# Ten pair tiles instead of eleven, under a newly written order table

## The chip, the cores and the metric

The kernel runs on one core of a Trainium2 chip. The metric is the device time of one execution in microseconds (us); lower is better. Five engines work side by side: PE (matrix products), DVE (vector operations), ACT (casts, copies, activations), POOL (almost unused here) and SP (which issues the DMA transfers).

## The reference

The input is 2048 rows of width 640 in float32. A layer of attention and a gated feed-forward network (FFN) are applied one after the other, each ahead of a residual sum:

```
h  = x + attention(layernorm(x)) @ wo       # 32 heads of 20; each row looks at 8 rows: itself and 2, 4, ... 14 back
h2 = h + (silu(n @ w_gate) * (n @ w_up)) @ w_down      # n = layernorm(h); 640 -> 1728 -> 640
```

## The kernel before

The rows are cut into four blocks of 512 (b = 0 to 3). Every float32 factor is split into a high and a low part (ACT casts the high part, DVE subtracts to get the low one), and each product is three passes of matmuls over them. So each operand costs DVE work before PE can use it.

Attention has no matmul for its logits and sums: the 16 pairs of block and head group are done on DVE. K, V and Q leave PE, are evicted by ACT into a staging tile `st` (L698), written to DRAM scratch (`ksc`, `vsc`, `qsc`, L711 to L727), and loaded back row-shifted into `kv` and `pq` (L742 and L747). DVE then multiplies (L755, L795), reduces (L760) and folds (L804), and SP writes the result to `osc` (L817).

The FFN's 1728 columns are 14 tiles of 128 (the last has 64). In the "classic" form a tile of one block is 30 matmuls of 512 columns for gate and up (L976; 15 for the last tile), SiLU on ACT (L1014), a product on DVE (L1015), a split (L1005 and L1007 or L1009) and 15 matmuls for the way down (L991). For blocks 0 and 1 all tiles are classic. Block 0 stores the low parts of the weights in DRAM (`lsc`, L967), and blocks 1 and 2 load them back (L962), so that DVE doesn't subtract again (L952).

Blocks 2 and 3 share work. A "pair tile" computes gate and up of both blocks at once with sums and differences of blocks and weights: 54 matmuls (L1164) in place of 60, and 13 DVE operations more (L1129 to L1201). The first `early` tiles and tile 13 are classic in both blocks. The next eight are "kept": their activations go to DRAM (`psc`), and a last stage (`products`, L1435) does their way down in a saving form. The others between are pair tiles too, and go down the classic way, in block 3 after the activations are loaded back (`kept_tile`, L1211).

```
        def pair(early):
            wo3(PR["wo"])
            paired = list(range(early, early + 2 * NP))
            others = [i for i in range(early, NF - 1) if i not in paired]
...
            ones = [*range(early), NF - 1]
...
                d.put(classic(2, i, first=n == 0))
...
            for i in others + paired:
                t = pair_tile(i, fn[0], lambda: d.pend and d.do(), i in paired, fn[0] == n0)
...
            for i in [NF - 1, *range(early)]:
                d.put(classic(3, i, new=True))
...
            for i in others:
                d.put(kept_tile(i))
```

`wo3` (L1262) is the attention's output projection for block 3, whose results ACT evicts (L1272). It stands between the classic tiles of block 2 and the sums for the pair tiles.

What each engine does next is not decided at run time. `Plan` records all operations with what they read and write; the table `ORDER` then says, in rows of (engine, index, count), in which order the recorded operations are issued. Each engine works off its own list in that order and waits by semaphores. All DMAs go through SP's one list.

Of the kernel before, what the change touches and what calls it, by code (L numbers as in the profile page):

```python
# [25 lines left out]
EARLY, NP = 2, 4  # L26
# [11 lines left out]
    (4, 2, 1), (4, 7, 1), (4, 4, 1), (2, 0, 1), (3, 1, 1), (3, 0, 1), (2, 1, 1), (1, 0, 1), (1, 10, 1), (2, 7, 1), (4, 3, 1), (2, 10, 1), (0, 0, 1), (4, 9, 1),  # L38
    (4, 8, 1), (0, 1, 1), (1, 6, 1), (0, 7, 1), (1, 1, 1), (0, 2, 2), (1, 4, 1), (4, 5, 1), (0, 4, 1), (0, 10, 1), (4, 6, 1), (1, 2, 1), (2, 8, 1), (0, 6, 1),
    (2, 2, 1), (1, 8, 1), (1, 12, 1), (1, 7, 1), (0, 11, 1), (2, 5, 1), (0, 12, 1), (4, 12, 1), (4, 10, 1), (2, 11, 1), (1, 3, 1), (0, 25, 2), (0, 13, 1),  # L40
    (0, 40, 1), (0, 27, 1), (2, 3, 1), (0, 28, 1), (2, 4, 1), (0, 41, 1), (0, 14, 2), (0, 5, 1), (1, 5, 1), (1, 14, 1), (2, 13, 1), (2, 6, 1), (0, 29, 1),
    (0, 16, 1), (0, 30, 1), (0, 42, 1), (4, 13, 1), (1, 9, 1), (1, 20, 1), (4, 0, 1), (4, 14, 1), (0, 17, 1), (0, 31, 1), (0, 18, 1), (1, 11, 1), (0, 19, 1),
    (0, 8, 2), (1, 16, 1), (2, 19, 1), (1, 15, 1), (0, 32, 1), (0, 20, 1), (1, 17, 1), (0, 21, 1), (0, 33, 1), (2, 12, 1), (1, 21, 1), (1, 18, 1), (0, 22, 1),
    (2, 9, 1), (0, 43, 1), (2, 15, 2), (0, 55, 1), (0, 44, 1), (1, 24, 1), (0, 56, 1), (1, 22, 1), (4, 15, 1), (0, 45, 1), (0, 57, 3), (1, 19, 1), (0, 34, 1),
    (4, 16, 1), (1, 23, 1), (0, 60, 2), (0, 46, 1), (0, 62, 1), (0, 47, 1), (0, 63, 1), (2, 20, 1), (0, 64, 2), (4, 1, 1), (1, 13, 1), (2, 14, 1), (0, 66, 1),
    (1, 25, 1), (0, 35, 1), (2, 21, 1), (0, 67, 1), (1, 26, 1), (0, 68, 1), (4, 45, 1), (0, 36, 1), (0, 23, 1), (4, 17, 1), (2, 22, 1), (0, 69, 1), (0, 48, 1),
    (0, 37, 2), (2, 23, 1), (0, 49, 2), (0, 39, 1), (2, 18, 1), (2, 17, 1), (0, 24, 1), (0, 51, 1), (4, 20, 1), (0, 52, 2), (1, 38, 1), (4, 18, 1), (1, 36, 1),
    (4, 19, 1), (1, 35, 1), (0, 54, 1), (1, 37, 1), (1, 63, 1), (4, 24, 1), (0, 70, 1), (4, 25, 2), (4, 21, 1), (4, 120, 2), (1, 59, 1), (1, 28, 1), (4, 119, 1),
    (2, 24, 1), (1, 29, 1), (0, 71, 1), (2, 25, 1), (0, 82, 1), (1, 68, 1), (4, 22, 1), (2, 28, 1), (1, 61, 1), (1, 39, 1), (1, 27, 1), (1, 31, 1), (2, 26, 1),
    (0, 73, 1), (1, 40, 1), (0, 72, 1), (4, 11, 1), (2, 30, 1), (1, 42, 1), (1, 41, 1), (2, 27, 1), (0, 84, 1), (1, 62, 1), (4, 27, 1), (0, 83, 1), (0, 75, 1),  # L50
    (4, 30, 1), (1, 70, 1), (4, 28, 1), (1, 64, 1), (2, 35, 1), (2, 53, 1), (4, 32, 1), (0, 74, 1), (2, 54, 1), (1, 65, 1), (4, 29, 1), (1, 33, 1), (1, 66, 1),
    (4, 31, 1), (0, 77, 1), (4, 23, 1), (2, 55, 1), (2, 32, 1), (0, 85, 1), (1, 34, 1), (2, 56, 1), (1, 60, 1), (2, 33, 1), (1, 32, 1), (4, 126, 1), (4, 125, 1),
    (1, 45, 1), (1, 43, 1), (1, 30, 1), (0, 76, 1), (2, 57, 1), (4, 33, 1), (1, 69, 1), (2, 31, 1), (2, 36, 1), (1, 46, 1), (4, 124, 1), (2, 29, 1), (1, 48, 1),
    (1, 67, 1), (0, 86, 1), (2, 58, 1), (2, 60, 1), (0, 78, 1), (4, 122, 1), (2, 59, 1), (2, 61, 1), (4, 123, 1), (1, 50, 1), (1, 44, 1), (4, 68, 1), (0, 79, 1),
    (1, 47, 1), (1, 198, 1), (2, 62, 2), (1, 199, 1), (2, 64, 1), (1, 49, 1), (1, 52, 1), (2, 65, 1), (1, 105, 1), (0, 80, 1), (2, 66, 1), (4, 34, 1), (2, 37, 1),
    (1, 51, 1), (1, 71, 1), (2, 67, 1), (1, 106, 1), (2, 68, 1), (1, 54, 1), (1, 107, 1), (4, 35, 1), (2, 34, 1), (4, 36, 1), (1, 53, 1), (0, 81, 1), (0, 88, 1),
    (1, 72, 1), (1, 108, 1), (2, 69, 1), (4, 128, 1), (2, 70, 1), (4, 130, 1), (2, 38, 1), (1, 109, 2), (4, 39, 1), (2, 71, 1), (4, 127, 1), (4, 137, 1),
    (1, 111, 1), (2, 39, 1), (0, 87, 1), (1, 58, 1), (1, 112, 1), (4, 37, 1), (1, 56, 1), (1, 55, 1), (2, 72, 1), (4, 139, 1), (4, 138, 1), (4, 38, 1), (0, 89, 1),
    (2, 41, 1), (1, 57, 1), (4, 69, 1), (4, 43, 1), (1, 74, 1), (4, 71, 1), (2, 73, 2), (1, 77, 1), (4, 40, 1), (2, 75, 2), (1, 75, 1), (4, 131, 1), (2, 77, 1),
    (4, 72, 1), (2, 78, 2), (4, 70, 1), (1, 78, 1), (0, 90, 1), (1, 73, 1), (4, 42, 1), (1, 200, 1), (2, 80, 1), (1, 79, 1), (4, 44, 1), (1, 80, 1), (4, 132, 1),  # L60
    (4, 129, 1), (2, 82, 1), (1, 201, 1), (0, 91, 2), (4, 41, 1), (4, 46, 1), (4, 133, 1), (4, 73, 1), (1, 76, 1), (2, 83, 1), (1, 81, 1), (2, 81, 1), (1, 82, 1),
    (0, 94, 1), (2, 84, 1), (4, 323, 1), (1, 84, 1), (2, 85, 2), (1, 83, 1), (2, 87, 1), (4, 85, 1), (0, 95, 1), (2, 88, 1), (4, 140, 1), (4, 135, 1), (1, 116, 1),
    (2, 89, 1), (0, 93, 1), (1, 85, 1), (4, 324, 1), (1, 86, 1), (2, 90, 2), (4, 51, 1), (1, 87, 1), (4, 50, 1), (1, 113, 1), (2, 40, 1), (4, 48, 1), (1, 114, 1),
    (0, 96, 1), (2, 92, 1), (4, 49, 1), (4, 136, 1), (1, 117, 1), (2, 44, 1), (4, 47, 1), (1, 115, 1), (2, 43, 1), (1, 118, 1), (2, 42, 1), (0, 98, 1), (1, 92, 1),
    (1, 88, 2), (0, 97, 1), (2, 93, 1), (0, 99, 1), (2, 46, 1), (4, 134, 1), (1, 90, 1), (1, 95, 1), (1, 93, 1), (4, 56, 1), (2, 94, 2), (4, 143, 1), (1, 91, 1),
    (2, 96, 1), (1, 96, 1), (1, 135, 1), (2, 45, 1), (0, 100, 1), (4, 55, 1), (4, 150, 3), (1, 94, 1), (2, 97, 2), (4, 147, 1), (4, 53, 1), (2, 99, 1), (1, 202, 1),
    (1, 136, 1), (4, 54, 1), (2, 100, 1), (1, 203, 1), (2, 102, 1), (4, 52, 1), (0, 111, 1), (0, 101, 1), (4, 141, 1), (4, 144, 1), (1, 137, 1), (2, 103, 2),
    (2, 101, 1), (2, 105, 1), (1, 100, 1), (4, 149, 1), (1, 99, 1), (2, 106, 1), (1, 139, 1), (0, 103, 1), (4, 57, 1), (2, 107, 1), (4, 58, 1), (0, 102, 1),
    (1, 98, 1), (1, 97, 1), (1, 102, 1), (4, 142, 1), (0, 105, 1), (1, 103, 1), (2, 108, 1), (4, 61, 1), (4, 145, 1), (4, 59, 1), (1, 104, 1), (4, 60, 1),
    (0, 112, 1), (2, 109, 1), (1, 101, 1), (1, 123, 1), (0, 104, 1), (4, 146, 1), (1, 121, 1), (1, 141, 1), (2, 110, 1), (0, 106, 1), (4, 64, 1), (1, 144, 1),  # L70
    (2, 111, 1), (4, 66, 1), (4, 62, 2), (4, 67, 1), (0, 107, 1), (1, 119, 1), (2, 112, 1), (1, 145, 1), (2, 113, 1), (1, 125, 1), (4, 65, 1), (1, 124, 1),
    (0, 113, 1), (4, 156, 1), (1, 146, 1), (4, 148, 1), (4, 165, 1), (4, 163, 1), (2, 49, 1), (1, 120, 1), (0, 110, 1), (4, 158, 1), (2, 114, 2), (1, 126, 1),
    (4, 74, 1), (1, 138, 1), (1, 142, 1), (2, 116, 1), (4, 154, 1), (2, 50, 1), (2, 117, 1), (0, 115, 1), (4, 164, 1), (2, 48, 1), (4, 157, 1), (4, 167, 1),
    (4, 75, 1), (1, 128, 1), (4, 325, 1), (4, 153, 1), (1, 127, 1), (0, 108, 1), (2, 118, 1), (1, 134, 1), (2, 119, 2), (1, 140, 1), (1, 122, 1), (4, 78, 1),
    (1, 133, 1), (0, 109, 1), (1, 130, 1), (4, 155, 1), (4, 76, 1), (1, 148, 1), (4, 326, 1), (0, 114, 1), (1, 204, 1), (4, 77, 1), (2, 122, 1), (1, 131, 1),
    (1, 143, 1), (1, 147, 1), (4, 79, 1), (1, 205, 1), (2, 121, 1), (1, 132, 1), (4, 160, 1), (0, 117, 1), (2, 123, 1), (4, 161, 1), (2, 47, 1), (0, 120, 1),
    (1, 129, 1), (1, 151, 1), (2, 51, 1), (2, 124, 2), (2, 52, 1), (4, 159, 1), (0, 116, 1), (2, 126, 1), (1, 152, 1), (0, 118, 1), (4, 331, 1), (4, 83, 1),
    (0, 119, 1), (2, 127, 1), (1, 154, 1), (1, 153, 1), (2, 128, 1), (4, 162, 1), (2, 129, 1), (1, 149, 1), (4, 332, 1), (4, 166, 1), (2, 130, 1), (0, 123, 1),
    (1, 150, 1), (2, 131, 1), (4, 82, 1), (0, 122, 1), (1, 156, 1), (1, 155, 1), (4, 81, 1), (4, 169, 1), (2, 132, 3), (4, 168, 1), (2, 135, 1), (4, 327, 1),
    (2, 136, 2), (4, 176, 1), (4, 170, 1), (2, 138, 1), (4, 178, 1), (4, 171, 1), (4, 177, 1), (4, 80, 1), (0, 121, 1), (1, 162, 1), (4, 87, 1), (2, 139, 1),  # L80
# [1557 lines left out]
```

## Time and profile before

| | us |
|---|---|
| median of 3 runs | 847.01 (845.80 to 847.99) |
| profiled execution, whole time | 847.86 |
| its span, first to last instruction | 845.8 |
| first matmul starts / last matmul ends, from the span's start | 1.9 / 842.5 |
| PE busy (x4037 matmuls) | 833.5 |
| DVE busy (x974) | 753.7 |
| ACT busy | 431.9 |

A busy PE is not PE at its peak: a matmul's record is longer than the distance to the next one, since matmuls overlap. The profile's rows give instructions by line, engine, operation and tile, with the busy time, the mean ns of one, and the idle time before them with what ended it.

### The profile page before, as it was taken

What the parts mean: (1) busy time and instruction counts of PE and PEld (TensorE: products, weight loads), DVE (VectorE), ACT (ScalarE), POOL (GpSimd) and SP (SyncE); (2) the same over time, 40 slices, a digit from 0 to 9 for tenths busy, and PEclk for the clock granted to TensorE, in tenths of its full rate; (3) what the DMA queues carried; (4) which work ended last, traced back from release to release, by engine and by line L of the source; (5) the groups of instructions that cost most, each with busy time, mean ns of one, the idle gap of its engine ahead of it and who ended that gap; (6) DMA issues with size and microseconds to landing.
All of it is one profiled execution on the core that took longest, in us unless ns stands there. A gap on an engine that the chain in (4) does not pass through costs nothing.

```text
span 845.8 us, 11075 instructions
## 1 busy us (share of the span) xinstructions
PE 833.5 (99%) x4037; PEld 713.4 (84%) x4037; DVE 753.7 (89%) x974; ACT 431.9 (51%) x804; POOL 2.8 (0%) x13
## 2 busy tenths in 40 slices
PE   8999999999999999999999999999999999999998
PEld 6888888889978788888888888888788888887998
DVE  6499999999998999999999999999986756667996
ACT  7755466253772443468345339467933232335550
POOL 0000000000000000000000000000000000000000
PEclk9999999999999999999999999999999999999999
DMA  7896978757779897679989989876322223268002
GB/s 256 224 246 172 283 203 236 217 142 227 187 216 282 271 283 235 222 218 275 328 265 299 283 278 283 247 268 241 120 90 75 88 82 100 81 227 323 1 33 93
DMA packets 89158, 173.35 MB, mean 205 GB/s; under 512 B 34464, under 2 KB 51200, under 8 KB 88464
## 3 DMA queue, kind: packets, MB, share of 16 engines
q1 hardware_dynamic: 89104, 172.66, 66.8%
q8 instruction: 31, 0.51, 0.2%
q14 instruction: 23, 0.19, 0.1%
HBM read 125.09 MB, written 47.16 MB: 204 GB/s over the span
## 4 chain that ended last, share of the span: by engine, by line
PE 78%; DVE 9%; DMA 8%; ACT 2%; issue 1%; SPq 1%; DVEq 0%; ACTq 0%
PE bank L691 18%; PE bank L976 18%; PE bank L1164 15%; PE bank L991 13%; PE bank L1435 6%; PE bank L888 5%; PE bank L1262 2%; DMA kv<-ksc 2%; DVE pq L795 1%; DMA pq<-qsc 1%; DMA vsc<-st 1%; DVE pq L755 1%; DMA lsc<-rb 1%; DVE rb L952 1%; DMA psc<-fa 1%
## 5 line engine op out<-in xcount | busy, mean ns | idle before, releaser
L976 PE MATMUL bank<-shb,rb 128*128 128x512 f32 x885 | 212.5, 390 | 1.9 <-DVE fa L1015 1.5
L976 PEld LDWEIGHTS bank<-shb,rb 128*128 128x128 f32 x885 | 165.1, 188 | 37.5 <-DVE fa L1015 2.4
L991 PE MATMUL bank<-rb,acts 128*128 128x512 f32 x464 | 122.5, 391 | 0.5 <-DVE acts L1009 0.5
L991 PEld LDWEIGHTS bank<-rb,acts 128*128 128x128 f32 x464 | 86.5, 188 | 18.4 <-DVE acts L1009 0.9
L755 DVE TENSOR_TENSOR pq<-kv,pq 128x2560 f32<-128x2560 f32 x32 | 90.2, 2820 | 6.4 <-DMA pq<-qsc 3.0
L804 DVE TENSOR_TENSOR pq<-pq 128x1280 f32<-128x1280 f32 (+2 forms) x96 | 89.4, 931 | 1.8
L795 DVE TENSOR_TENSOR pq<-kv,pq 128x2560 f32<-128x2560 f32 x32 | 90.2, 2820 | 0.7
L760 DVE TENSOR_REDUCE pq<-pq 128x128 f32<-128x2560 f32 x32 | 90.0, 2812 | 0.4
L698 ACT ACTIVATE st<-bank,fa 128x128 f32<-128x128 f32 (+3 forms) x120 | 50.5, 476 | 64.4 <-PE bank L691 37.7
L888 PE MATMUL bank<-ra 128*128 128x320 f32 x360 | 56.0, 309 | 0.0
L888 PEld LDWEIGHTS bank<-ra 128*128 128x128 f32 x360 | 54.3, 188 | 1.7 <-ACT fa L891 0.2
L691 PE MATMUL bank<-ra,sha 128*128 128x480 f32 (+2 forms) x240 | 54.4, 382 | 0.7 <-DVE sha L639 0.5
L691 PE MATMUL bank<-ra,shb 128*128 128x512 f32 (+1 forms) x240 | 52.5, 378 | 0.9 <-ACT st L698 0.9
L691 PE MATMUL bank<-rb,sha 128*128 128x512 f32 (+1 forms) x240 | 52.9, 379 | 0.0
L691 PE MATMUL bank<-rb,shb 128*128 128x512 f32 (+1 forms) x230 | 51.5, 379 | 0.0
L691 PEld LDWEIGHTS bank<-ra,shb 128*128 128x128 f32 x240 | 44.9, 188 | 7.8 <-ACT st L698 1.2
L691 PEld LDWEIGHTS bank<-ra,sha 128*128 128x128 f32 x240 | 44.3, 188 | 8.0 <-DVE sha L639 0.9
L691 PEld LDWEIGHTS bank<-rb,sha 128*128 128x128 f32 x240 | 44.8, 188 | 6.5
L691 PEld LDWEIGHTS bank<-rb,shb 128*128 128x128 f32 x230 | 42.9, 188 | 6.2
L957 ACT CAST rb<-fa 128x1280 fp32r<-128x1280 f32 (+1 forms) x32 | 38.9, 1215 | 17.9 <-DMA fa<-in_ffn_dram 14.4
L1014 ACT ACTIVATE fa<-bank 128x512 f32<-128x512 f32 x30 | 17.9, 598 | 51.1 <-PE bank L976 41.5
L952 DVE TENSOR_TENSOR rb<-fa,rb 128x640 fp32r<-128x640 f32 (+1 forms) x52 | 41.9, 814 | 1.1 <-ACT rb L957 1.1
(213 smaller groups left out, 1309.0 us busy)
## 6 DMA issues: line engine op xcount, KB each, us to landing
fa<-in_ffn_dram SPq DMA_DIRECT2D x33, 960.0 KB, 5.3
kv<-ksc SPq DMA_DIRECT2D x32, 440.0 KB, 6.2
kv<-vsc SPq DMA_DIRECT2D x32, 440.0 KB, 7.7
rb<-lsc SPq DMA_DIRECT2D x15, 640.0 KB, 6.4
lsc<-rb SPq DMA_DIRECT2D x13, 640.0 KB, 7.6
rb<-lsc SPq DMA_DIRECT2D x19, 320.0 KB, 4.4
ksc<-st SPq DMA_DIRECT2D x32, 160.0 KB, 3.5
pq<-qsc SPq DMA_DIRECT2D x16, 320.0 KB, 7.0
```

The lines of the kernel that those rows point to most:

```text
L691: T.matmul(banks[bk][:, 0:n], l, r_(wq(g, w, c) + shift, n), start=(p, c) == first_mm, stop=(p, c) == last_mm)
L698: P.add("ACT", act(m) + 0.06, lambda: A.activation(stage_t()[:, o : o + NJ * m].rearrange("p (t j c) -> p t j c", j=NJ, c=w)[:, :, j, :], ...
L755: P.add("DVE", dve(2560), lambda: V.tensor_tensor(pq(PROD, 2560).rearrange("p (j w c) -> p j w c", j=2, w=W), window(ko, 2 * jp), pq(qo + ...
L760: P.add("DVE", dve(2560), lambda: V.tensor_reduce(logits(lo)[:, :, 16 * jp : 16 * jp + 16].rearrange("p h n -> p n h"), pq(PROD, 2560).rea ...
L795: V.tensor_tensor(pq(PROD, 2560).rearrange("p (j n d) -> p j n d", j=2, d=DH), bass.AP(tensor=v.tensor, offset=v.offset, ap=[list(v.ap[0]) ...
L804: V.tensor_add(dst(v), v[:, :, 0:m, :], v[:, :, m : 2 * m, :])
L888: T.matmul(banks[bk][:, 0:320], l, r_(m, 320), start=p == 0 and c == 0, stop=p == 2 and c == NC - 1)
L952: low(640, lambda E, o=o: E.tensor_sub(ws(t, lo + o, 640)[p0:], fa[p0:, raw + o : raw + o + 640], ws(t, hi + o, 640)[p0:].bitcast(F32)), [ ...
L976: T.matmul(banks[bk], ws(wt, gu + 1280 * w + wid * c + col, 128), x(a, c), start=p == 0 and c == 0, stop=p == 2 and c == NC - 1)
L991: T.matmul(banks[k], l, m, start=first and p == 0, stop=stop and p == len(passes) - 1)
L1164: T.matmul(banks[bk], ws(wt, o + 2048 * w + 128 * k, 128), xv_[k](a), start=first and p == 0 and k == 0, stop=stop and p == 2 and k == n - ...
L1435: T.matmul(banks[bk0 + tp][:, 0:HN], v[:, 512 * a + 128 * tp : 512 * a + 128 * tp + 128], v[:, 1024 + HN * w : 1024 + HN * w + HN], start= ...
```

## The change

The constant `EARLY` goes from 2 to 3, and the table `ORDER` is written anew for all engines. No other line differs.

```diff
-EARLY, NP = 2, 4
+EARLY, NP = 3, 4
@@ ORDER, rows of (engine, index, count)
-    (4, 2, 1), (4, 7, 1), (4, 4, 1), (2, 0, 1), (3, 1, 1), (3, 0, 1), (2, 1, 1), (1, 0, 1), (1, 10, 1), (2, 7, 1), (4, 3, 1), (2, 10, 1), (0, 0, 1), (4, 9, 1),
...
```

With `EARLY` 3, tile 2 is classic in block 2 and in block 3; the kept tiles are 3 to 10 instead of 2 to 9, and the others are 11 and 12 instead of 10 to 12. So one pair tile and one `kept_tile` go, and two classic tiles come. Counted over the whole program:

| | before | after |
|---|---|---|
| matmuls (all of 512 columns where they differ) | 4037 | 4043 |
| of them L1164 / L976 | 594 / 960 | 540 / 1020 |
| DVE instructions | 974 | 964 |
| DMAs issued by SP | 553 | 553 |
| loads of FFN weights: L938 of 1920 columns / of 640 | 33 / 3 | 34 / 2 |
| loads from `lsc`: 1280 / 640 columns | 15 / 19 | 16 / 20 |
| `psc` stores L1202 and loads L1211 | 11 + 3 | 10 + 2 |

Three places of the order follow. In the rows, `bank` is a PSUM bank, `ra`, `rb` and `shb` hold split operands, `acts` the activations, `fa` raw loads and single-precision values.

PE, at the end of block 2's classic tiles, where the matmuls of `wo3` (L1262) stand; before:

```order
L1262 MATMUL bank7_77<-ra_66 128x320 x9
L991 MATMUL bank3_73<-rb_67,acts_2071 128x512 x2
L1262 MATMUL bank7_77<-ra_66 128x320 x18
L1262 MATMUL bank0_70<-ra_66 128x320 x6
L1262 MATMUL bank7_77<-ra_66 128x320 x9
L1262 MATMUL bank0_70<-ra_66 128x320 x6
L1262 MATMUL bank7_77<-ra_66 128x320 x6
L976 MATMUL bank6_76<-shb_68,rb_67 128x512 x5
```

and now:

```order
L976 MATMUL bank5_75<-shb_68,rb_67 128x512 x10
L1262 MATMUL bank7_77<-ra_66 128x320 x9
L976 MATMUL bank6_76<-shb_68,rb_67 128x512 x10
L1262 MATMUL bank7_77<-ra_66 128x320 x9
L976 MATMUL bank6_76<-shb_68,rb_67 128x512 x5
```

Gate and up matmuls of a classic tile now stand between the groups of `wo3`, which followed each other before.

SP, in block 0's FFN, where the K rows of the ninth of the 16 attention pairs are loaded (`kv<-ksc`); before:

```order
L938 DMA fa_65<-in_ffn_dram 128x1920
L817 DMA osc_81<-pq_93 32x5x64
L747 DMA kv_69<-vsc_79 64x1760
L747 DMA kv_69<-ksc_78 64x1760
L742 DMA pq_93<-qsc_80 128x640
L747 DMA kv_69<-ksc_78 64x1760
L967 DMA lsc_84<-rb_67 128x640
```

and now:

```order
L967 DMA lsc_84<-rb_67 128x1280
L817 DMA osc_81<-pq_89 32x5x64
L938 DMA fa_65<-in_ffn_dram 128x1920
L747 DMA kv_69<-ksc_78 64x1760 x2
L742 DMA pq_89<-qsc_80 128x640
```

The two K loads, which had the Q load between them, now stand together ahead of it. In the table, 16 matmuls stood between the later K load and the multiplication that reads it (L755); now 52 do.

ACT, at the start of the program; before:

```order
L451 ACT_TABLE_LOAD
L451 ACTIVATE fa_65<-fa_65 128x1
L486 ACTIVATE fa_65<-fa_65 128x640
L487 ACTIVATE fa_65<-fa_65 128x1
L491 ACTIVATE fa_65<-fa_65 128x640
L638 CAST sha_124<-bank7_77 128x512
```

and now:

```order
L662 ACT_TABLE_LOAD
L662 CAST ra_66<-fa_65 128x480
L451 ACT_TABLE_LOAD
L451 ACTIVATE fa_65<-fa_65 128x1
L662 CAST ra_66<-fa_65 128x480
L638 CAST sha_118<-bank7_77 128x512
L486 ACTIVATE fa_65<-fa_65 128x640
```

A cast of the first weights now stands first, with a second load of the activation table behind it, and the statistics of an input tile (L486 to L491) stand behind the first cast of transposed input (L638).

465 rows, old and new, of the table ORDER are left out of this document.

## The prediction

> **What bounds the kernel now.** I read the page's first part, then the windows, the groups by form, the waits, the chain, and the timeline at each wait of PE. The page:
>
> ```profile
> span 845.8 us, 11075 instructions
> PE 833.5 (99%) x4037; PEld 713.4 (84%) x4037; DVE 753.7 (89%) x974; ACT 431.9 (51%) x804; POOL 2.8 (0%) x13
> ```
>
> PE looks full and DVE nearly so. The windows (25 us each: busy us and count of PE, PEld, DVE, ACT, POOL, then clock, DMA share, GB/s) show that these are two regimes:
>
> ```profile
> 450.00:475.00 25.00, 25.00 (x126) 21.68 (x125) 24.69 (x24) 12.73 (x18) 0.00 (x0) 1.00 0.96 315
> 525.00:550.00 25.00, 25.00 (x112) 20.70 (x111) 24.47 (x22) 13.75 (x21) 0.00 (x0) 1.00 0.88 269
> 650.00:675.00 25.00, 25.00 (x112) 20.67 (x112) 15.88 (x27) 7.76 (x12) 0.00 (x0) 1.00 0.22 80
> ```
>
> Up to about 600 us DVE is busy 98% of the time beside PE; in the pair tiles it is busy for 64%. The granted clock is 1.00 in both. Whether a "busy" PE loses time is read from its pace, in the chain (start, us, what, count):
>
> ```profile
> 344.60 2.57 PE bank L976 x10
> 347.85 2.27 PE bank L976 x10
> ...
> 724.61 25.85 PE bank L1164 x114
> ...
> 797.19 44.88 PE bank L1435 x306
> ```
>
> A 512-column matmul takes 25.85/114 = 0.2268 us where nothing disturbs it, a 320-column one 44.88/306 = 0.1467. The ten at 344.60 took 2.57 instead of 2.27: 0.30 us that no idle time shows. PE's groups between 240 and 600 us (count, then busy, mean ns, idle):
>
> ```profile
> L976 PE MATMUL bank<-shb,rb 128*128 128x512 f32 x885 | 212.5, 390 | 1.9 <-DVE fa L1015 1.5 <-ACT rb L957 0.3
> L991 PE MATMUL bank<-rb,acts 128*128 128x512 f32 x331 | 88.0, 391 | 0.0
> L888 PE MATMUL bank<-ra 128*128 128x320 f32 x240 | 37.8, 309 | 0.0
> L991 PE MATMUL bank<-acts,rb 128*128 128x512 f32 x83 | 23.7, 391 | 0.0
> L1262 PE MATMUL bank<-ra 128*128 128x320 f32 x120 | 19.6, 313 | 0.6 <-ACT fa L1272 0.5
> ```
>
> 1299 x 0.2268 + 360 x 0.1467 = 347.4 us; 51 smaller ones in four more rows add 5.4 (36 of 128 columns at 0.067, 15 of 448 at 0.200, on the straight line through the two paces). That is 352.8 of 360 us: 7.2 us are lost here. The 114 pair-tile matmuls lost nothing. So the loss lies where DVE has no slack. What PE waited for in all (total, times, longest):
>
> ```profile
> PE bank L976 <- DVE fa L1015: 1.8, 2, 1.5
> PE bank L548 <- ACT st L698: 1.1, 1, 1.1
> PE bank L691 <- ACT st L698: 0.9, 1, 0.9
> PE bank L1262 <- ACT fa L1272: 0.5, 1, 0.5
> PE bank L991 <- DVE acts L1009: 0.5, 1, 0.5
> ```
>
> Each of these costs some 0.16 us more, since a record (0.39) covers that much beyond the pace (0.227). The longest began with a transfer (first the median us to landing of its kind, then the one):
>
> ```profile
> kv<-ksc SPq DMA_DIRECT2D x32, 440.0 KB, 6.2
> ```
>
> ```profile
> 260.58 13.84 DMA kv<-ksc
> ...
> 274.50 2.82 DVE L755 TENSOR_TENSOR pq<-kv,pq 128x2560 f32<-128x2560 f32 x1 [2.66 <-DMA kv<-ksc]
> ...
> 280.71 2.58 PE L976 MATMUL bank<-shb,rb 128*128 128x512 f32 x10 [1.50 <-DVE fa L1015]
> ```
>
> K rows landed after 13.84 us, DVE stood 2.66 us before its multiplication (L755), the FFN product L1015 queued behind it came late, and PE lost 1.50. DVE, with no lead over PE, passes each late landing on.
>
> **The change, part by part.**
>
> *PE work.* Six more matmuls: 6 x 0.2268 = +1.36 us, all on the path. This is sure.
>
> *DVE cover.* The lists, counted up to the first L1164, have 2881 PE instructions before and 2929 now: 48 matmuls, 10.9 us, moved ahead of the pair tiles (30 of L976, 18 of L991). DVE's lists up to the first L1179 have 674 and 676.
>
> ```profile
> L1141 DVE TENSOR_TENSOR rb<-fa,rb 128x1024 fp32r<-128x1024 f32 x6 | 7.3, 1218 | 0.0
> L1129 DVE TENSOR_TENSOR rb<-fa,rb 128x640 fp32r<-128x640 f32 x6 | 4.9, 819 | 0.0
> L1129 DVE TENSOR_TENSOR rb<-fa,rb 128x384 fp32r<-128x384 f32 x6 | 3.3, 550 | 0.0
> L1139 DVE TENSOR_TENSOR fa<-fa 128x256 f32<-128x256 f32 x11 | 4.6, 417 | 0.2
> L1195 DVE TENSOR_TENSOR fa<-fa 128x512 f32<-128x512 f32 x11 | 7.5, 685 | 0.2
> L1015 DVE TENSOR_TENSOR fa<-bank,fa 128x512 f32<-128x512 f32 x30 | 20.4, 680 | 0.7 <-PE bank L976 0.7
> ```
>
> The classic tile in block 2 costs DVE one L1015 and one split like it: 1.4 us (its low parts are loaded). So DVE gains 10.9 - 1.4 = 9.5 us of lead over PE by the first pair tile. It builds up on the way: ahead of the 20th L1015 DVE's list has one L795, two L804 and one L811 less, and one L1007 more. Over the program DVE sheds the 13 rows of a pair tile (1.22 + 0.82 + 0.55 + 2 x 0.42 + 8 x 0.69 = 8.9 us) and gets two L1015 and one L952 (2.2): -6.7 us, of which only the order in time matters.
>
> What that lead is worth is bounded by the losses: between 0 and 7.2 us in 240 to 600. The waits there that are not DVE's are L548, L976 on ACT and L1262: 1.1 + 0.3 + 0.5 and 3 x 0.16 = 2.4. The DVE wait is 1.5 + 0.16 = 1.7; the remaining 3.1 is late starts like that at 344.60. I take off the 1.7, 2.5 of the 3.1, and 0.4 at L1262, whose wait on ACT now has gate and up matmuls in between: -4.6, nearer the upper bound, since the pair-tile stretch with DVE at 64% lost nothing.
>
> *After the pair tiles* PE waited 0.5 for L1009 and 0.3 for L1015 (1.1 with the hidden part). DVE comes with the same lead: -0.6, between 0 and -1.1. The classic tile in block 3 adds an L1015 and an L952 here; the pair tile's 54 L1164 matmuls, with 8.9 us of DVE, are gone, so DVE stays covered.
>
> *Attention stage.* The L691 wait followed one late V store:
>
> ```profile
> ACT st L698 <- DMA vsc<-st: 6.8, 1, 6.8
> ```
>
> K and V transfers have more room in the new table (the smallest count of matmuls between a K load and its reader is 17, before 0). It may avoid 0 to 1.1; I take -0.5, half.
>
> *Start.* ACT's second table load stands behind a cast that waits for weights:
>
> ```profile
> 0.79 1.28 ACT L451 ACT_TABLE_LOAD   x1 [0.79 <-PEq L1627]
> ...
> 4.51 0.74 ACT L486 ACTIVATE fa<-fa 128x640 f32<-128x640 f32 x1 [2.22 <-DMA fa<-in_x_dram]
> ...
> 8.18 1.22 ACT L662 CAST ra<-fa 128x480 fp32r<-128x480 f32 x2 [0.51 <-DMA fa<-in_wqkv_dram]
> ...
> 236.58 1.28 ACT L780 ACT_TABLE_LOAD   x1
> 237.88 0.42 ACT L780 ACTIVATE pq<-pq 128x256 f32<-128x256 f32 x1
> ```
>
> The load costs 1.28 and hid in ACT's idle start before; now it can delay PE by all of it. Against that, weights issued earlier may save the 0.51. I take +0.6, between -0.5 and +1.3, as part of ACT's 2.22 us of waiting for x can still cover it. [...]
>
> *SP and transfers.* SP issues 553 DMAs as before, and ACT's 31 table loads stay 31. But block 2's new classic tile loads earlier what is bulky:
>
> ```profile
> fa<-in_ffn_dram SPq DMA_DIRECT2D x33, 960.0 KB, 5.3
> rb<-lsc SPq DMA_DIRECT2D x15, 640.0 KB, 6.4
> ```
>
> 960 + 640 + 320 KB more come in the stretch where the DMA share is 0.88 to 0.96. I cost it at nothing, because the lead of DVE and ACT's 50% of idle time hide it; without that cover it is 1.92 MB at 290 GB/s = 6.6 us. Next to be late is ACT's cast of raw weights.
>
> *The sum* on the profiled execution: 847.86 + 1.36 - 4.6 - 0.6 - 0.5 + 0.6 = 844.1. That execution lies 0.85 above its median (847.01), and the K landing of 13.84 us (the others: 6.2) is part of its losses, so I credit half of the 0.85: **843.7 us**, 0.39% below the median. About 0.3% (2.5 us) can be told from no change here.
>
> **The rivals.**
>
> *PE alone decides.* The lost time goes with the order of banks and evictions, not with DVE. Then 847.0 + 1.36 + 0.6 = 849.0. For it: PE is at 99%, and ACT ended three of the five waits shown. Against it: the undisturbed pair tiles, with the same ACT. [...]
>
> *The waits come back.* The new lists are as tight for ACT and for transfers, and half of the 5.7 us returns elsewhere: 847.0 + 1.36 + 0.6 - 2.9 = 846.1. A table laid out for given landings does nothing for others, and three runs of before already spread over 2.2 us.
>
> *Transfers become the bound (slower).* At the raw weight loads of block 1 and 2 ACT already waits:
>
> ```profile
> ACT rb L957 <- DMA fa<-in_ffn_dram: 14.4, 6, 5.4
> ```
>
> Only 0.3 of it reached PE. If the 1.92 MB lengthen these landings, PE waits for L957. With nothing else saved and a third of the 6.6 us on PE: 849.0 + 2.2 = 851.2. It decides from 0.6 us of such waits on, if no other loss falls.
>
> **How the numbers follow.** Forecast 0.57 (own range 840.5 to 844.4: 3.2 below, if 6 of 7.2 us and the start are saved too), PE alone 0.10, waits come back 0.20, transfers 0.13. Faster 0.57, within 0.3% (844.5 to 849.5) 0.30, slower 0.13. The range 840.5 to 849.0 leaves out the transfers' case and the tails.
>
> **What would show it.** Right: PE x4043; matmul loss between 240 and 610 us of 2 to 4 us by the same count; no wait of PE on L1015 above 0.5 us; DVE waiting for PE's banks before 600 us; pair tiles at 0.2268; first L691 in a row without gaps within 1.3 us of 17.25. Wrong: waits of L976 on L957 in sum above 1 us, or DVE still at 98% with L1015 ending PE's waits, or a start over 2 us late.

## The result: 0.65% slower, and the profile after

The changed kernel takes 852.17 us (median of 15 runs, 847.91 to 855.80) against 846.35 us of the kernel before beside it (15 runs, 844.21 to 849.08). The ratio is 1.0065, 95% interval 1.0049 to 1.0081. The forecast was 843.7 (840.5 to 849.0). The profiled execution took 852.36 us.

The page of the changed kernel, its first part:

```profile
span 850.6 us, 11091 instructions
PE 834.8 (98%) x4043; PEld 715.0 (84%) x4043; DVE 750.7 (88%) x964; ACT 432.2 (51%) x802; POOL 2.8 (0%) x13
```

PE has its six more matmuls, and is idle for longer. The windows, as before:

```profile
450.00:475.00 25.00, 22.40 (x103) 18.02 (x102) 22.18 (x21) 10.47 (x16) 0.00 (x0) 1.00 1.02 290
525.00:550.00 25.00, 24.76 (x110) 20.06 (x108) 24.62 (x27) 16.51 (x24) 0.00 (x0) 1.00 0.89 252
650.00:675.00 25.00, 25.00 (x112) 20.68 (x111) 17.97 (x29) 8.55 (x14) 0.00 (x0) 1.00 0.35 111
```

In the first one PE did 103 matmuls where it did 126, and DVE, which was busy for 24.69 us, for 22.18. What PE waited for over the whole program:

```profile
PE bank L976 <- ACT fa L1014: 2.8, 3, 1.6
PE bank L976 <- DVE fa L1015: 2.7, 2, 1.6
...
PE bank L888 <- ACT fa L891: 1.2, 1, 1.2
PE bank L976 <- DMA rb<-lsc: 1.0, 1, 1.0
```

No single wait is long, and no one engine ends them all. All of these lie between 438 and 535 us, in block 1's FFN, where the last attention pairs still run. What the other engines waited for in 400 to 560 us (the kernel before had 1.3 us in the first of these rows, and none of the second and third):

```profile
ACT rb L957 <- DMA fa<-in_ffn_dram: 11.2, 2, 7.1
...
DVE pq L787 <- ACT pq L781: 4.0, 1, 4.0
...
DVE pq L755 <- DMA osc<-pq: 3.3, 1, 3.3
```

ACT's timeline at the longest one (start, duration, then in brackets the idle time before it and what ended it), with DVE's and PE's rows behind it:

```profile
503.34 1.26 ACT L957 CAST rb<-fa 128x1280 fp32r<-128x1280 f32 x1 [7.15 <-DMA fa<-in_ffn_dram]
```

```profile
505.18 0.43 DVE L787 TENSOR_TENSOR pq<-pq 128x256 f32<-128x256 f32 x1 [3.98 <-ACT pq L781]
```

```profile
506.06 2.47 PE L888 MATMUL bank<-ra 128*128 128x320 f32 x15 [1.19 <-ACT fa L891]
511.51 1.42 PE L976 MATMUL bank<-shb,rb 128*128 128x512 f32 x5 [1.15 <-DVE fa L1015]
```

Here is one late raw load and its whole train. ACT stands for 7.15 us before the cast. Behind it on ACT's list are the eviction L891 and the attention copy L781. PE waits for the first; DVE waits for the second, and L1015 behind it comes late for PE. None of this appears as a wait of PE on L957.

To see where time goes, I take PE's start times minus the work done until then (0.2268 us for each 512-column matmul, 0.1467 for each 320-column one), and compare two traces at the same amount of work. The changed kernel was 3.5 us ahead at 390 us of work, 6.1 behind at 534 (so 9.6 lost in that middle stretch), and 3.2 behind at the end, besides the 1.36 us of added matmuls.

Median landing times (last column, us) of transfers issued between 400 and 540 us of the span, before:

```profile
fa<-in_ffn_dram SPq DMA_DIRECT2D x11, 960.0 KB, 5.1
rb<-lsc SPq DMA_DIRECT2D x12, 640.0 KB, 6.2
kv<-vsc SPq DMA_DIRECT2D x8, 440.0 KB, 6.9
```

and after:

```profile
fa<-in_ffn_dram SPq DMA_DIRECT2D x11, 960.0 KB, 8.2
rb<-lsc SPq DMA_DIRECT2D x11, 640.0 KB, 8.6
kv<-vsc SPq DMA_DIRECT2D x8, 440.0 KB, 11.0
```

The transfers are no more (37.87 MB moved there against 39.42), and these three kinds take 1.4 to 1.6 times as long to land. Not all do: the K loads (`kv<-ksc`) went from 5.6 to 5.9 us.

### The profile page after: what moved, and what is told of

The parts are those of the page before. It is cut to its first block, busy times and chain, and to the rows that moved or that the text cites. A ratio compares the mean times of both kernels' runs of the same rounds, so it can differ in the third digit from the quotient of the medians.

```text
span 850.6 us, 11091 instructions
## 1 busy us (share of the span) xinstructions
PE 834.8 (98%) x4043; PEld 715.0 (84%) x4043; DVE 750.7 (88%) x964; ACT 432.2 (51%) x802; POOL 2.8 (0%) x13
## 5 line engine op out<-in xcount | busy, mean ns | idle before, releaser
L976 PE MATMUL bank<-shb,rb 128*128 128x512 f32 x915 | 221.9, 391 | 7.2 <-ACT fa L1014 2.8
L976 PEld LDWEIGHTS bank<-shb,rb 128*128 128x128 f32 x915 | 170.3, 188 | 45.0 <-ACT fa L1014 4.0
L755 DVE TENSOR_TENSOR pq<-kv,pq 128x2560 f32<-128x2560 f32 x32 | 90.2, 2819 | 11.2 <-DMA pq<-qsc 7.5
L804 DVE TENSOR_TENSOR pq<-pq 128x1280 f32<-128x1280 f32 (+2 forms) x96 | 89.6, 933 | 2.1
L795 DVE TENSOR_TENSOR pq<-kv,pq 128x2560 f32<-128x2560 f32 x32 | 90.3, 2821 | 0.7
L698 ACT ACTIVATE st<-bank,fa 128x480 f32<-128x480 f32 (+3 forms) x120 | 51.2, 475 | 44.9 <-PE bank L691 33.2
L888 PE MATMUL bank<-ra 128*128 128x320 f32 x360 | 55.7, 309 | 1.2 <-ACT fa L891 1.2
L888 PEld LDWEIGHTS bank<-ra 128*128 128x128 f32 x360 | 54.1, 188 | 2.9 <-ACT fa L891 1.6
L957 ACT CAST rb<-fa 128x1280 fp32r<-128x1280 f32 (+1 forms) x34 | 40.6, 1198 | 19.5 <-DMA fa<-in_ffn_dram 15.4
L1005 ACT CAST acts<-fa 128x512 fp32r<-128x512 f32 x36 | 22.3, 619 | 48.7 <-DVE fa L1015 44.6
```

The source lines that it names most:

```text
L698: P.add("ACT", act(m) + 0.06, lambda: A.activation(stage_t()[:, o : o + NJ * m].rearrange("p (t j c) -> p t j c", j=NJ, c=w)[:, :, j, :], ...
L755: P.add("DVE", dve(2560), lambda: V.tensor_tensor(pq(PROD, 2560).rearrange("p (j w c) -> p j w c", j=2, w=W), window(ko, 2 * jp), pq(qo + ...
L795: V.tensor_tensor(pq(PROD, 2560).rearrange("p (j n d) -> p j n d", j=2, d=DH), bass.AP(tensor=v.tensor, offset=v.offset, ap=[list(v.ap[0]) ...
L804: V.tensor_add(dst(v), v[:, :, 0:m, :], v[:, :, m : 2 * m, :])
L888: T.matmul(banks[bk][:, 0:320], l, r_(m, 320), start=p == 0 and c == 0, stop=p == 2 and c == NC - 1)
L976: T.matmul(banks[bk], ws(wt, gu + 1280 * w + wid * c + col, 128), x(a, c), start=p == 0 and c == 0, stop=p == 2 and c == NC - 1)
```

## The experiments

The two programs record the same operations up to the pair tiles; EARLY changes only what comes behind. So either table can be followed up to a place, and the other from there on, each engine skipping what it has done. Three stretches were used: up to 393 us of PE's work, the middle (393 to 534), and the rest. The place where one table's order gives way to the other's is called a seam. Medians of the kernel before beside the runs were 846.5 to 847.0.

### Which stretch loses

```diff
 e1: order of the middle, in the changed kernel (EARLY = 3)
-the changed table's rows
+the rows of before
 e2: order up to 393 us, in the kernel before (EARLY = 2)
-the rows of before
+the changed table's rows
 e3: order of the middle, in the kernel before (EARLY = 2)
-the rows of before
+the changed table's rows
 e4: the kernel before up to 534 us, from there on the changed kernel (EARLY = 3)
```

> The changed kernel (EARLY 3, ten pair tiles), but the middle stretch of the program (393 to 534 us of PE's work: block 1's FFN beside the last attention pairs) in the order of the kernel before. By the two traces the changed kernel gains 4.0 us up to the middle, loses 10.1 in it and gains 1.6 behind it. Theory (the middle stretch's order loses the time): 840.7 us. Rival 1 (late landings that follow whatever stands ahead, so that the middle's order is innocent): about 852. Rival 2 (the extra classic tile and its transfers): about 848.5.

> The kernel before (EARLY 2, eleven pair tiles), with only the first stretch (up to 393 us of PE's work) in the changed kernel's order. Theory (gain of the first stretch is real and is kept where the middle stretch is in the order of before): 846.35 - 4.0 = 842.4 us. Rival 1 (the gain of the first stretch is only borrowed, and given back in the middle whatever order that has): 846 to 852. Rival 2 (the extra classic tile): 842.4 too.

> The kernel before (EARLY 2), with only the middle stretch (393 to 534 us of PE's work) in the changed kernel's order. Theory (the middle stretch's order loses 10.1 us by itself): 846.35 + 10.1 = 856.4 us. Rival 1 (landings follow what stands ahead): about 846.4. Rival 2 (the extra classic tile): about 846.4.

> The order of before up to 534 us of PE's work, then the changed kernel: EARLY 3, ten pair tiles, and its order for the rest. Theory (tile and order behind the middle gain 1.6 us): 844.8 us. Rival 1: the same, 844.8. Rival 2 (the extra classic tile and its 1.92 MB of earlier loads cost the time): about 852.

Measured: e1 850.78 (ratio 1.0050, 1.0034 to 1.0067), e2 851.69 (1.0058, 1.0041 to 1.0076), e3 856.92 (1.0133, 1.0112 to 1.0154), e4 844.69 (0.9980, 0.9971 to 0.9990).

e3 and e4 came within 0.5 us of the theory: the middle's order loses time by itself, and the last stretch, with the extra classic tile and its loads, gains 1.8. The tile change was not at fault. In e3's trace PE stops at four of the six places where the changed kernel's PE stops for over 0.9 us here (461, 465, 505 and 510 us there; 461, 464, 503 and 510 in e3's), and ACT's longest wait for a raw load is 7.7 us against 7.1: the list makes these stalls, not chance. But e3 came so near to 856.4 partly by luck. In its trace (3.2 us above its median) 7.6 us are lost in the middle and 5.7 at its far seam, and the changed kernel has no such loss behind the middle.

e1 and e2 missed by about 10 us. Both lose 7 us at one stop at the seam, 393 us of work (e1's PE):

```profile
417.63 7.47 PE L976 MATMUL bank<-shb,rb 128*128 128x512 f32 x20 [4.16 <-DVE fa L1015]
```

Behind the 4.16 us of waiting the granted clock stays at 0.50 for 5.7 us more, which costs another 2.8 (see the last section). The changed table had put one attention multiplication (L795, 2.83 us of DVE) off beyond that place; the rows of before then have it ahead of L1015, and PE pays. The next run moved the cut to where DVE's lists agree.

```diff
 e5: as e1, with the cut at 406 us of PE's work instead of 393
```

> As the kernel whose middle stretch is that of before (EARLY 3), but with the cut at 406 us of PE's work instead of 393, a place where DVE has done the same steps in both tables, so that no attention multiplication (an L795 with its folds, some 8 us of DVE) is left over at the seam. In the trace of the changed kernel PE is 3.7 us ahead of before at that place. Theory (the first stretch's gain is real, the 8 us lost at the seam were that one postponed multiplication): 846.4 - 3.7 - 1.6 = 841.1 us. Rival (the first stretch's gain is a debt that the middle has to pay in any order): 844.7 or more, as with the last stretch alone.

Measured: 849.56 (1.0034, 1.0015 to 1.0052). Again a stop at the seam, 3.78 us of PE waiting for L1007. At this cut a K load was still to be issued (the changed table has it 21 operations later), and DVE did the multiplication that reads it (L755, after 0.69 us of waiting) ahead of L1007. At both places where I cut, the changed order had something of the attention chain still to do. Its lead of PE was partly borrowed from that chain, so the rival is nearer.

### SP's list

```diff
 e6: the changed kernel, between 406 and 534 us
-SP's list as it is
+SP's transfers in the order of before
 e8: the kernel before, between 406 and 534 us
-SP's list as it is
+SP's transfers in the changed order
```

> The changed kernel; only SP's list between 406 and 534 us of PE's work stands in the order that it has before (four transfers are moved back by one or two places, where they would wait for each other in a circle). PE, ACT and DVE keep the changed lists. Theory (SP's order, with loads of raw weights late and in bunches, loses the time): 852.2 - 8 = 844 us. Rival (the computing engines' lists lose it: attention work put off on DVE, groups of PE in another order): 852, or more, since SP then fits nobody.

> The kernel before; only SP's list between 406 and 534 us of PE's work stands in the changed kernel's order. Theory (SP's order loses the time): 846.4 + 8 = 854 us. Rival (the computing engines' lists lose it): 846 to 848.

Measured: e6 874.71 (1.0305, 1.0278 to 1.0331), e8 869.43 (1.0265, 1.0246 to 1.0284). Both lose over 20 us: neither list of SP suits the other's engines. This decides nothing between the theories beyond that, but prices a misfit of SP's list (in e6, one wait of 10.7 us for L1015).

```diff
 e7: the changed kernel, SP's list at 474 to 489 us of its trace
 L873 fa<-osc
+L938 fa<-in_ffn_dram
 L817 osc<-pq
 L962 rb<-lsc
 L873 fa<-osc
+L938 fa<-in_ffn_dram
 L742 pq<-qsc
 L747 kv<-ksc
-L938 fa<-in_ffn_dram
 L747 kv<-ksc
 ...
 L747 kv<-vsc
-L938 fa<-in_ffn_dram
```

> The changed kernel; two loads of raw FFN weights (L938, 960 KB each, read by ACT's L957 casts at 491.0 and 503.3 us in its trace, after 4.1 and 7.2 us of waiting) stand 6 places and 8 places earlier in SP's list. Theory (the waits of ACT for these two loads are passed on to PE through L891, L1014 and L1015 behind them on ACT's list): 852.2 - 1.2 - 1.1 - 1.0 - 3 x 0.16 = 848.4 us, the L957 waits near 0. Rival (the DMA engines are full there, so that what is pulled ahead only delays the K and V rows): 852, with DVE's L755 or L795 waiting instead.

Measured: 847.13 (1.0002, 0.9985 to 1.0019), 5.0 us less than the changed kernel's 852.17. Waits of ACT in 400 to 560 us:

```profile
ACT rb L957 <- DMA fa<-in_ffn_dram: 0.6, 1, 0.6
```

The 11.2 us are gone, DVE's 4.0 us before L787 too, and PE's stops at 492, 505 and 510 us with them (0.3 left). Two places in SP's list are worth most of the loss; more than the 3.8 expected.

```diff
 e9: the changed kernel, between 393 and 540 us of PE's work
-SP's list as it is
+SP's transfers as soon as each can start, the one needed first ahead, none over 26 us before its need
```

> The changed kernel; SP's transfers between 393 and 540 us of PE's work are put in another order, by when each can start and when its reader needs it in the changed kernel's own trace (a transfer is issued as soon as it can start, the one needed first ahead, none over 26 us before its need). PE, ACT and DVE keep the changed lists. Theory (SP's list loses the 10.1 us of the middle: stores of attention results that wait for DVE stand ahead of loads, and loads start late): 852.2 - 8 = 844 us, the attention multiplications less than 4 us later than before at the end of the stage instead of 12.5. Rival (the computing engines' lists lose it): 847, no better than with the two raw loads alone.

Measured: 850.20 (1.0046, 1.0029 to 1.0063): far from 844. Nearly all of the stretch is smooth, and one stop is left. PE's, ACT's and SP's rows:

```profile
463.80 0.73 PE L976 MATMUL bank<-shb,rb 128*128 128x512 f32 x1 [4.37 <-ACT fa L1014]
```

```profile
462.85 0.41 ACT L877 CAST ra<-fa 128x256 fp32r<-128x256 f32 x1 [7.38 <-DMA fa<-osc]
463.16 0.59 ACT L1014 ACTIVATE fa<-bank 128x512 f32<-128x512 f32 x1
```

```profile
436.59 0.33 SPq L938 DMA_DIRECT2D fa<-in_ffn_dram  x1
437.02 0.45 SPq L747 DMA_DIRECT2D kv<-vsc  x1
437.61 0.48 SPq L962 DMA_DIRECT2D rb<-lsc  x1
438.15 0.63 SPq L747 DMA_DIRECT2D kv<-vsc  x1
438.87 2.05 SPq L1529 DMA_DIRECT2D out_dram<-h  x4
442.98 6.09 SPq L817 DMA_DIRECT2D osc<-pq  x4
449.37 1.19 SPq L747 DMA_DIRECT2D kv<-ksc  x2
```

Four stores of 40 KB needed 6.09 us to be issued. Ahead of them stand exactly eight transfers. The first four of these landed at 442.82, 444.76, 446.81 and 448.74; the four stores were issued at 442.98, 444.77, 446.82 and 448.76. So each store was issued 0.01 to 0.16 us after the landing of the transfer eight places ahead (a raw load, V rows, low parts, V rows).

### Less work for DVE, fewer bytes

```diff
 e10 (the changed kernel) and e11 (the kernel before)
-V.tensor_add(dst(v), v[:, :, 0:m, :], v[:, :, m : 2 * m, :])
+c = 80 if m == 4 else GC
+V.tensor_add(dst(v)[..., 0:c], v[:, :, 0:m, 0:c], v[:, :, m : 2 * m, 0:c])
 e12 (the changed kernel), L962
-Q.dma_start(ws(t, at_, m).bitcast(F32), lsc[i, :, o : o + m])
+Q.dma_start(ws(t, at_, m // 4).bitcast(F32), lsc[i, :, o : o + m // 4])
```

> The changed kernel with less DVE work: the first fold of each attention product (L804, 1280 elements, 1.48 us) is done on half its columns (0.81 us), so that 32 x 0.67 = 21 us of DVE are left out over the attention stage, some 13 of them behind 240 us; the attention sums lack that part. Theory of transfers (SP's list holds loads back and the waits for them pass to PE): most of the loss stays, since ACT's L957 waits stay: 848 us. Rival (DVE has no slack, each late landing costs because DVE can't catch up): 852.2 - 9 = 843 us.

> The kernel before with the same work left out (half of the first fold, 21 us of DVE in all). The prediction put 7.2 us of PE's losses in 240 to 600 us down to DVE without slack, 4.6 of which a lead of DVE should bring back: by that 846.4 - 4.6 = 841.8 us. Rival (PE's order of banks and evictions alone decides): 846.4.

> The changed kernel; the loads of the weights' low parts (L962) bring a quarter of their columns, so 36 loads carry 4.2 instead of 17 MB (the products use what stood in the rest before). No transfer changes its place in the list. Theory (SP's order: loads wait behind stores for DVE, whatever their size): 850 us. Rival (the DMA engines are full, and landings of 8 to 15 us come from the bytes in flight): the landings fall to those of before or below, 852.2 - 8 = 844 us.

Measured: e10 846.62 (0.9993, 0.9974 to 1.0013), e11 844.22 (0.9969, 0.9958 to 0.9980), e12 849.15 (1.0019, 1.0002 to 1.0037).

e11 bounds the forecast's main term. With 21 us of DVE's work gone (the attention sums then lack that part), over twice the counted lead of 9.5, the kernel before gains 2.5 us, not 4.6. Nor does much of it lie where the forecast looked for it: between 235 and 600 us of PE's work, e11's trace loses 6.1 us and that of before 7.0. In e10 the same cut gains 5.5, yet ACT still waits for raw loads:

```profile
ACT rb L957 <- DMA fa<-in_ffn_dram: 13.1, 2, 7.5
```

So the loads are late for their own reason, and DVE's spare time absorbs part of it. In e12, with 12.8 MB less, 10.5 us of these waits stay too; the 3.0 us that it gains say that bytes under way have some part. Neither theory has it alone.

### Stores off SP's list

```diff
 e13 (the changed kernel), e14 (the kernel before), e15 (e4's order), e16 (e9's order), L817
-Q.dma_start(
+G.dma_start(
     osc[b, jp, GC * g : GC * g + GC, q, :].rearrange("(f c) t -> c f t", c=32),
```

> The changed kernel; only the stores of the attention results (L817, 40 KB each, in sets of four that wait for DVE) are issued by POOL's own queue instead of SP's list. The traces show that SP never has more than eight transfers under way (a transfer is not issued before the one eight places ahead of it has landed), and that between 400 and 540 us SP stood still for this 5.4 us before and 22.7 us in the changed kernel. Theory (places in SP's list and its eight transfers under way hold the loads back): SP's stops fall to a third, and 852.2 - 8 = 844 us. Rival (the DMA engines are full, the bytes come no sooner): 850 or more.

> The kernel before with the same stores on POOL's queue. Theory (SP's stops cost what the middle loses; before has few of them): a gain of 1 us at most, 845.5. Rival (POOL's queue is better or worse in itself, whatever SP's list is): as much gained or lost as in the changed kernel.

> The order of before up to 534 us, the changed kernel's last stretch (EARLY 3), and the stores of the attention results on POOL's queue. Theory: 844.7 - 1 = 843.7 us. Rival (POOL's queue costs in itself): 846 or more.

> The changed kernel with SP's transfers of the middle ordered by need, and the stores of the attention results on POOL's queue. In the kernel without POOL one stall of 4.4 us was left, behind four such stores that were issued 2 us apart, each when the transfer eight places ahead had landed; the granted clock of 0.5 behind it cost 1.7 more. Theory (that stall goes): 850.2 - 6 = 844 us. Rival (osc loads and casts come late for another reason): 849 or more.

Measured: e13 847.90 (1.0027, 1.0010 to 1.0044), e14 848.20 (1.0012, 1.0000 to 1.0024), e15 845.96 (0.9993, 0.9977 to 1.0009), e16 850.14 (1.0035, 1.0022 to 1.0048).

On POOL's queue the stores cost about a microsecond where SP's list was sound (e14 against before 1.5, e15 against e4 1.3, by medians; up to 1 less was expected of both) and gain 4.3 in the changed kernel. The 847.90 lie between the 844 of the theory and the rival's 850 or more. The changed kernel's excess over the kernel before falls from 0.65% to 0.27%. Against e14, the kernel before with the same stores on POOL, nothing is left that can be told from noise: the ratios differ by 0.15% with overlapping intervals, and e13's median is the lower one. What SP waited for in 400 to 540 us, in the changed kernel:

```profile
SPq L817 <- DVE pq L811: 10.7, 3, 6.5
...
SPq L817 <- DMA fa<-in_ffn_dram: 5.7, 3, 3.7
...
SPq L817 <- DMA rb<-lsc: 4.4, 4, 2.0
...
SPq L817 <- DMA kv<-vsc: 4.1, 2, 2.2
```

The first row is 8.5 in the kernel before; the second is absent there. With the stores on POOL none of these stands in front of a load, and the middle loses 4.6 us in e13's trace instead of 9.6. The rest is the two raw loads, not moved here (10.9 us of waits on L957).

e16 gained nothing: its one stop, 4.77 us for L1014, is e9's. So the stores' places on SP's list are not the cause of that one. Two runs moved the cast instead.

```diff
 e17 (on e7) and e18 (on e9): ACT's list at 461 us of the changed kernel's trace
-L877 ra<-fa
 L1014 fa<-bank
 L780 pq<-pq
-L877 ra<-fa
-L877 ra<-fa
 L1005 acts<-fa
 L781 pq<-pq
+L877 ra<-fa
+L877 ra<-fa
+L877 ra<-fa
```

> The changed kernel with the two raw loads earlier, and in ACT's list three casts of block 1's attention results (L877) four places later, so that the SiLU (L1014) for which PE's next L976 waits stands ahead of the first of them and not behind. No transfer and no other list changes. Theory (a cast that waits for a transfer blocks the ready SiLU behind it): PE's wait for L1014 at 461 us (1.1, with what a record hides 1.3) goes: 847.1 - 1.3 = 845.8 us. Rival (the casts are needed just as early, by PE's L888, so the wait only moves there): 847.1.

> The changed kernel with SP's transfers of the middle ordered by need, and the same three casts four places later in ACT's list. In the kernel by need alone one stall was left between 400 and 540 us, 4.4 us at 459, behind the first of these casts, and 1.7 us at half clock after it. Theory (the wait for a transfer costs only through what stands behind the waiting cast on ACT's list): both go, 850.2 - 6.2 = 844.0 us. Rival (the attention results are late on the path themselves): PE waits as long for L888 instead, 850.

Measured: e17 846.91 (1.0010, 0.9991 to 1.0029), e18 850.06 (1.0039, 1.0016 to 1.0061). Neither gains. In e18's trace the stop at 459 us is gone and one of 3.24 us stands at 475, through DVE:

```profile
466.94 1.29 DVE L878 TENSOR_TENSOR ra<-fa,ra 128x512 fp32r<-128x512 f32 x2 [3.73 <-ACT ra L877]
...
477.78 0.69 DVE L1015 TENSOR_TENSOR fa<-bank,fa 128x512 f32<-128x512 f32 x1
```

The rival holds, though the wait is not at L888 as it had it: the attention results are late themselves, and whichever list meets them first stands. In the changed trace the 13th pair's first multiplication by K (L755) starts at 430.42 us, 5.0 later than before, though PE is 3.7 ahead in its work; at the 16th pair it is 13.6 later. What that remaining part would need, earlier K loads and an earlier L795 in DVE's list, was not tried.

## Why the prediction was wrong, step by step

**PE work: right.** x4043, and the pair tiles ran at 31.54/139 = 0.2269 us:

```profile
632.30 31.54 PE bank L1164 x139
```

**Start: better than taken.** The row without gaps started at 16.98 us (17.25 before). At 20 us of work the changed order was between 0.9 ahead and level in its traces, except e6's (1.5 behind), where I took +0.6. ACT's second table load (1.28 us at 4.98 in the changed kernel's, the next row 0.02 behind it) cost PE nothing that these traces show. (The forecast's list of PE's waits leaves out rows of the start, the longest of them L563 for POOL: 1.9 us before, 1.4 now. Its sum doesn't use them.)

**Attention stage and DVE cover: the gain was the luck of one execution, and borrowed.** By the first trace the changed kernel was 3.5 us ahead at 390 us. But the changed order's first stretch ran in ten profiles with SP's stores in place (after, e1, e2, e5, e6, e7, e9, e12, e17, e18), and there stood between 3.5 ahead and 1.0 behind the first trace of before, on average 1.3 ahead. The order of before ran in four (before, e3, e4, e8): from level to 2.2 ahead, on average 1.3 ahead. So with the stores on SP's list no gain of the first stretch is shown, in traces that spread over 4.5 us. (With the stores on POOL's queue the changed order was 2.9 to 5.2 us ahead there, e13 and e16 against e14 and e15; why stays open.) The forecast read 7.2 us of losses off an execution that was itself unlucky there, and took off only 0.4 us for that. The lead of 9.5 us was a count at the pair tiles; on the way it was made of attention steps not done yet (one L795, two L804, one L811 "less"). I called work put off a lead.

**After the pair tiles and at L1262: right in sign, too small.** I took off 1.0 and added 1.36 for the matmuls, +0.36 in all; e4 measured -1.8 in all, so some 3.2 gained instead of 1.0.

**SP and transfers: the step that failed.** "I cost it at nothing, because the lead of DVE and ACT's 50% of idle time hide it." The middle cost 9.6 us by the trace. With the first stretch at 0 and the last at -1.8, the medians' +5.8 leave 7.6 for it. Of these, e7's two moved loads alone bring back 5.0. I looked at bytes in the block-2 tile's loads, and not at the places of small stores and big loads in SP's list in block 1. ACT's idle time hides nothing when ACT stands in order before a cast whose load is late.

**The rivals.** *Transfers become the bound* gave 851.2 and came nearest, by luck, since place and cause were others: not the 1.92 MB of the new tile (e4 has them and is faster), and its sign, waits of L976 on L957, never showed. These waits reached PE as L1014, L891 and L1015. *PE alone decides* is refuted by e11: less DVE work does help, by 2.5 us. *The waits come back* (846.1) took half of the gain away; the runs lost all of it and 3.2 us beyond (852.2 against 849.0 with no gain at all). Counted as in the prediction, the loss between 240 and 600 us is 360 - 1280 x 0.2268 - 355 x 0.1467 - 4.9 (43 smaller ones) = 12.7 us, not 2 to 4.

The best version seen is e4: the order of before up to 534 us with ten pair tiles behind it, 844.69 us, 0.20% below the kernel before (0.10 to 0.29%).

## What to carry to other kernels

Where engines work off lists in order, cost a moved transfer by what stands in front of it: a small store that waits for a compute engine, or the transfer that holds its place under way, delays every load behind it (moving two loads gained 5.0 us in e7, moving the stores to another queue 4.3 in e13). A wait for a transfer shows under another name, at whatever stands behind the waiting instruction, so sum the waits of all engines in the stretch before calling an engine's idle time cover (here ACT waited 11.2 us at L957, and PE never there). A lead counted in instructions has to be checked for which work was put off to get it, and a loss read off one execution has to be seen in a second one before it is promised back.

## What the runs showed of the program and the hardware that was not expected

**Eight transfers under way.** In all 16 profiles with the stores on SP's list (409 transfers in each whose predecessor's landing is recorded), none was issued before the transfer eight places ahead had landed, while 75 (before) and 64 (after) were issued before the one seven places ahead had. SP's stops for this sum to about 5.4 us in 400 to 540 us before, 22.7 after, 14.4 in e7, without the quarter of the transfers whose predecessor's landing is not recorded. The limit is the program's own way of counting landings. The traces name the semaphore that each transfer signals: SP's use eight in strict turn, so that each of the 545 behind the first eight has that of the transfer eight places ahead, and 491 of them before and 481 after wait for it, in the transfer itself or in an instruction between it and the transfer ahead. Whether the hardware would take more under way is not shown.

**Half clock after short stops.** A stop of PE can cost more than itself. Behind e9's 4.37 us the granted clock (third number from the end) was:

```profile
462.00:464.00 2.00, 0.20 (x1) 0.20 (x2) 0.22 (x1) 1.14 (x3) 0.00 (x0) 0.98 1.11 423
464.00:466.00 2.00, 2.00 (x5) 1.55 (x6) 0.89 (x2) 1.99 (x4) 0.00 (x0) 0.50 1.01 424
466.00:468.00 2.00, 2.00 (x7) 1.56 (x6) 1.46 (x3) 1.98 (x4) 0.00 (x0) 0.67 0.98 402
```

About 3.4 us at 0.50 cost 1.7 us more. Over all profiles, all seven stops of more than 3.7 us had this with them, of 19 between 1.8 and 3.3 us nine, and of 30 between 1.0 and 1.8 us one (1.23 us, at the program's start). The clock records give each of these stretches as 3.41 us long, or as 6.83 or 13.65, twice and four times that; some begin while PE still stands. It cost 1.4 to 3.0 us each time. What decides whether a stop has such a stretch with it is not shown; its length alone does not, as ten of the 19 had none. Eleven of the changed kernel's fifteen runs have a mean clock of 0.995 to 0.998, while fifteen of before beside e1 have 0.998 to 1.000. One stretch of 3.41 us at 0.50 lowers the mean over 850 us by 0.002; by this estimate most of its runs have such stretches as well, which the profiled one (1.000 and none before its last matmul) does not show. That this makes its runs spread over 7.9 us, and those of before over 4.9, is not shown: the run with the shortest time has 0.998, and the three at 1.000 take 850.2 to 853.0 us.
